# A convolution-gated layer with an MLP on one core: the order of two first loads, and the cut of the last output tile

## The chip, the cores and the metric

The kernel runs on one core of a Trainium2 chip. The metric is the device time of one execution in microseconds (us); the lower, the better. Each version is timed in several runs and the median is given. One execution is also profiled: the profile's times are counted from the start of its span, and "the profiled execution" below means that one.

## The reference

The inputs are one sequence of 2048 tokens with 512 channels (`A_q`, `A_k`, `A_v`), four tap weights for each channel (`A_shift_k`, 512 x 4), a long filter for each channel (`A_ssm_k`, 512 x 2048), a skip weight for each channel (`A_ssm_D`) and two MLP matrices (512 x 1376 and 1376 x 512), all bf16.

```python
kv = (sum over t of shifted k * shift_k) * v          # four taps along the sequence
y  = causal long convolution of kv with ssm_k          # FFT of length 4096 in the reference
h  = x + layernorm(x) * (y + kv * ssm_D)
h2 = h + relu(layernorm(h) @ w1) @ w2                  # output, 2048 x 512
```

## The kernel before

The long convolution is done as two-stage Fourier transforms by TensorE: the filter and `kv` are turned into rows of the first stage, multiplied by small sine matrices, combined stage by stage, multiplied pointwise and transformed back. The MLP follows in four blocks of 512 tokens. The program is written in one order by hand, and each engine takes its instructions strictly in that order, so an instruction that waits holds all that stand behind it on the same engine. Loads and stores are issued by SyncE (SP) and by ScalarE (ACT); each has a DMA queue of its own, and both queues run on the same 16 DMA engines.

**The start.** SP issues the load of the tap weights `wsh` (line 123: 4 KB, in 512 runs of 8 bytes), then the load of the long filter `sk` (line 124: 2 MB, in 512 runs of 4 KB), then eight transposing loads of k and v, alternately (lines 134 to 137). ACT issues two loads of `ssm_D` (line 128) and then loads its table of sines. TensorE (PE) runs 28 matmuls of zeros (line 156, `psz`), whose result nobody reads; they fill the time until `sk` is there. Then come 32 transposes of the filter (line 284, `pst`), in `to_rows` for h = 0 to 3. The first of them waits for `sk`. They are written as 8, 8, 8, 4 and 4; the results are copied out of PSUM (line 287 on ACT, line 289 on VectorE, DVE): the first, third and fourth group by ACT, the second and the fifth by DVE. The fifth group waits for DVE's copy of the second. Behind them stand the taps (line 335, `pkv`), matmuls against diagonal matrices `wdiag`, and the first Fourier stage (line 300).

**What stands behind the tap weights.** DVE's line 191 casts `wsh` to `wf` and waits for its load. Behind it on DVE, in this order: the phases of the small sine tables (lines 44 and 46, eight instructions in all; the fifth waits for nothing of the load but reads what POOL wrote), casts of the first table (lines 210 to 215), the phases of the large table (lines 222 and 220), small constants (lines 229 to 233), and then the copy of the second transpose group (line 289). On ACT: two sines (line 147) that need the phases, 16 products that make `wdiag` (line 204; they need `wf`), one more sine, and then the copies of line 287. POOL's line 246 reads `ssm_D`.

**The end.** `mlp2` (lines 664 to 681) makes one output tile of 128 tokens at a time: 11 matmuls (line 674), a DVE instruction that scales and adds (line 676), and a store issued by ACT (line 679). The last tile (t = 15) is made in two halves of 256 columns, each with its own 11 matmuls, DVE instruction and store. A store's destination is described as 4 x 32 rows.

Of the kernel before, what the change touches and what calls it, by code (L numbers as in the profile page):

```python
# [15 lines left out]
P = 128  # L16
# [40 lines left out]
def kernel(  # L57
# [13 lines left out]
    nc = tc.nc  # L71
    _, S, D = A_q.shape
# [3 lines left out]
    NT = 16  # L76
# [26 lines left out]
    def view(at, n, dt, t=E):  # L103
        return t[:, at:at + n].bitcast(dt)

    def small(shape, dt):
        n = math.prod(shape) * (2 if dt == BF16 else 4) // 4
        v = view(taken[0], n, dt)
        taken[0] += n
        return v.rearrange("p (a b) -> p a b", a=shape[0]) if len(shape) == 2 else v  # L110
# [9 lines left out]
    tsn = G[:, 2048:4096].rearrange("p (a b) -> p a b", a=32)  # L120

    wsh = consts.tile([P, DC, KS], BF16, name="wsh")
    nc.sync.dma_start(out=wsh[:], in_=A_shift_k.rearrange("(r p) j -> p r j", p=P))
    nc.sync.dma_start(out=sk, in_=A_ssm_k.rearrange("(c p) t -> p c t", p=P))
    draw = small([DC * P], BF16)
    for dp in range(2):
        src = bass.AP(tensor=A_ssm_D.tensor, offset=A_ssm_D.offset, ap=[[0, 1], [1, DC * P]])
# [536 lines left out]
    def mlp2(sc, hook=None):  # L664
        h1T = h1s[sc]
        for i in range(4):
            t = 4 * sc + i
            o = ob[t % 3]
            w = D // 2 if t == NT - 1 else D
            for d0 in range(0, D, w):  # L670
                ps2 = psm.tile([P, D], F32, tag="ps", name="ps2m")[:, 0:w]
                for fc in range(NFC):
                    ksz = min(P, DFF - fc * P)
                    nc.tensor.matmul(out=ps2, lhsT=h1T[:ksz, fc, i * P:(i + 1) * P], rhs=w2[:ksz, fc, d0:d0 + w],  # L674
                                     start=(fc == 0), stop=(fc == NFC - 1))
                nc.vector.scalar_tensor_tensor(out=o[:, d0:d0 + w], in0=ps2, scalar=rstd2[:, t, :], in1=xh[sc][:, i, d0:d0 + w],  # L676
                                               op0=ALU.mult, op1=ALU.add)
                dst = bass.AP(tensor=out_d.tensor, offset=out_d.offset + t * D + d0, ap=[[16 * D, 4], [64 * D, 32], [1, w]])
                nc.scalar.dma_start(out=dst, in_=o[:, d0:d0 + w])
            if hook is not None:  # L680
                hook(i)

# [20 lines left out]
    def next_norm(q):  # L703
# [7 lines left out]
        return hook  # L711

    mlp2(0, next_norm(2))
    inv2(2, psz)
    ec_wrap(3)
    mlp1(1, lambda fc: ec_sins(3, (fc // 3,)) if fc in (1, 4, 7, 10) else None)
    stats(xh[1], mv2, rstd2, 1)
    gate(2)
    mlp2(1, next_norm(3))
    inv2(3, psz)  # L720
    mlp1(2)
    stats(xh[2], mv2, rstd2, 2)
    gate(3)
    mlp2(2)
    mlp1(3)
    stats(xh[3], mv2, rstd2, 3)
# [32 lines left out]
```

## Time and profile before

| | us |
|---|---|
| median of 3 runs | 208.73 |
| lowest and highest | 208.56, 209.94 |
| the profiled execution's own time | 208.83 |
| span of its profile | 206.4 |
| PE busy | 198.7 (96%) |
| DVE busy | 141.8 (69%) |
| ACT busy | 117.3 (57%) |
| last matmul ends, by the chain of waits | 202.03 |
| last DVE instruction | 202.05 to 202.53 |

The span is what the profiler saw of the program; 2.4 us of the profiled execution's time lie around it. The profile's chain of waits follows the work that ended last back from the end; its pieces, put in order of time, tell which engine's work the end hung on at each moment. The timeline gives an instruction's start, its duration and, in brackets, how long its engine had been idle before it and what ended that. "SPq" and "ACTq" are the issuing of DMAs by these two engines.

### The profile page before, as it was taken

What the parts mean: (1) busy time and instruction counts of PE and PEld (TensorE: products, weight loads), DVE (VectorE), ACT (ScalarE), POOL (GpSimd) and SP (SyncE); (2) the same over time, 40 slices, a digit from 0 to 9 for tenths busy, and PEclk for the clock granted to TensorE, in tenths of its full rate; (3) what the DMA queues carried; (4) which work ended last, traced back from release to release, by engine and by line L of the source; (5) the groups of instructions that cost most, each with busy time, mean ns of one, the idle gap of its engine ahead of it and who ended that gap; (6) DMA issues with size and microseconds to landing.
All of it is one profiled execution on the core that took longest, in us unless ns stands there. A gap on an engine that the chain in (4) does not pass through costs nothing.

```text
span 206.4 us, 4344 instructions
## 1 busy us (share of the span) xinstructions
PE 198.7 (96%) x1733; PEld 138.3 (67%) x1741; DVE 141.8 (69%) x246; ACT 117.3 (57%) x190; POOL 69.5 (34%) x118
## 2 busy tenths in 40 slices
PE   8999999998999999999999999999999999999991
PEld 2575556877899998899998944466444844444450
DVE  5989898698689989997743775899079742261131
ACT  5776789787687787777692068403950065026300
POOL 7963801991555699232003032042202010002000
PEclk9999999999999999999999999999999999999997
DMA  5999990001600000035515999999906717110011
GB/s 147 353 205 168 203 162 6 0 5 21 258 0 0 3 0 3 0 105 102 96 35 180 229 224 121 212 145 134 114 17 118 161 25 91 42 56 17 0 51 51
DMA packets 47818, 19.91 MB, mean 96 GB/s; under 512 B 42710, under 2 KB 46264, under 8 KB 47800
## 3 DMA queue, kind: packets, MB, share of 16 engines
q1 hardware_dynamic: 44144, 16.15, 42.4%
q10 hardware_dynamic: 3656, 3.51, 6.0%
q8 instruction: 13, 0.21, 0.4%
q14 instruction: 5, 0.04, 0.1%
HBM read 7.02 MB, written 2.10 MB: 44 GB/s over the span
## 4 chain that ended last, share of the span: by engine, by line
PE 94%; DVE 2%; ACT 1%; issue 1%; ACTq 0%
PE ps1m L658 18%; PE ps2m L674 18%; PE psi L555 11%; PE u L433 8%; PE us L443 8%; PE ps L300 8%; PE pz L646 7%; PE pkv L335 7%; PE psz L156 4%; PE pst L284 4%; DVE BK L450 1%; ACT ktu L423 1%; ACT BX L273 0%; DVE BK L312 0%; ACT BK L315 0%
## 5 line engine op out<-in xcount | busy, mean ns | idle before, releaser
L660 ACT ACTIVATE M<-ps1m 128x512 bf16<-128x512 f32 (+1 forms) x44 | 25.1, 595 | 49.4 <-PE ps1m L658 28.1
L674 PE MATMUL ps2m<-M 128*128 128x512 bf16 (+3 forms) x183 | 38.5, 366 | 0.2
L674 PEld LDWEIGHTS <-M 128*128 128x128 bf16 (+1 forms) x187 | 18.3, 98 | 19.9
L658 PEld LDWEIGHTS <-w 128*128 128x128 bf16 (+1 forms) x176 | 17.4, 100 | 19.9
L383 POOL TENSOR_TENSOR smc<-st 64x256 fp32r<-64x256 f32 x32 | 22.8, 731 | 13.6 <-PE us L443 12.8
L517 POOL TENSOR_SCALAR rstd<-mv 128x4 f32<-128x4 f32 x8 | 2.2, 277 | 70.1 <-DVE mv L515 70.1
L676 DVE SCALAR_TENSOR_TENSOR M<-ps2m,rstd,M 128x512 bf16<-128x512 f32 (+1 forms) x13 | 9.1, 705 | 22.6 <-PE ps2m L674 13.5
L450 DVE TENSOR_TENSOR BK<-u,ktu 128x512 fp32r<-128x512 f32 x32 | 20.6, 685 | 4.9 <-PE us L443 2.7
L555 PE MATMUL psi<-inv,BK 128*128 128x128 f32 x128 | 21.1, 255 | 0.0
L423 ACT COPY ktu<-u 128x512 f32<-128x512 f32 x32 | 18.0, 588 | 5.1 <-DVE BK L450 2.4
L555 PE MATMUL psi<-inv,BX 128*128 128x256 f32 x64 | 20.5, 338 | 0.1
L555 PEld LDWEIGHTS psi<-inv,BK 128*128 128x128 f32 x128 | 19.7, 197 | 0.0
L658 PE MATMUL ps1m<-M,w 128*128 128x512 bf16 (+1 forms) x88 | 19.3, 379 | 0.0
L658 PE MATMUL ps1m<-xT,w 128*128 128x512 bf16 (+1 forms) x88 | 19.3, 379 | 0.0
L433 PE MATMUL u<-BK,st 64*128 64x256 f32 x128 | 14.2, 303 | 0.0
L433 PE MATMUL u<-BX,st 64*128 64x256 f32 x128 | 13.0, 283 | 0.0
L555 PEld LDWEIGHTS psi<-inv,BX 128*128 128x128 f32 x64 | 12.1, 196 | 0.4 <-DVE BK L450 0.4
L513 DVE BATCH_NORM_STATS2 st<-M 128x6 f32<-128x512 bf16 x20 | 12.3, 677 | 0.0
L315 ACT CAST BK<-ps 128x512 fp32r<-128x512 f32 x16 | 9.3, 585 | 5.0 <-PE ps L300 3.4
L632 DVE TENSOR_TENSOR qT<-pz,qT 128x2048 bf16<-128x2048 f32 x2 | 4.6, 2291 | 10.7 <-DMA qT<-M 6.5
L443 PE MATMUL us<-BK,smc 128*128 128x256 f32 x64 | 10.8, 294 | 0.7 <-ACT BX L273 0.6
L450 DVE TENSOR_TENSOR BX<-us,kts 128x512 fp32r<-128x512 f32 x16 | 10.9, 685 | 0.8
(126 smaller groups left out, 405.5 us busy)
## 6 DMA issues: line engine op xcount, KB each, us to landing
E<-in_A_ssm_k_dram SPq DMA_DIRECT2D x1, 2048.0 KB
out_dram<-M ACTq DMA_DIRECT2D x15, 128.0 KB
w<-in_B_w_dram SPq DMA_DIRECT2D x1, 1376.0 KB
M<-in_B_w_dram ACTq DMA_DIRECT2D x1, 1280.0 KB
M<-in_A_q_dram SPq DMA_DIRECT2D x8, 128.0 KB
xh<-in_A_q_dram SPq DMA_DIRECT2D x4, 128.0 KB
xr<-in_A_q_dram SPq DMA_DIRECT2D x4, 128.0 KB
out_dram<-M ACTq DMA_DIRECT2D x2, 64.0 KB
```

The lines of the kernel that those rows point to most:

```text
L300: nc.tensor.matmul(out=pss[rp][:, gi // 2, :, gi % 2, :], lhsT=fl[rows, 2 * g:2 * g + 2, :].rearrange("p d n -> p (d n)"), rhs=f[rows].rea ...
L335: nc.tensor.matmul(out=ps[:, i, :], lhsT=wdiag[:, r0 + i, j, :], rhs=kT[c][:, r0 + i, 16 - j:CH + 16 - j], start=(j == 0), stop=(j == KS - 1))
L383: nc.gpsimd.tensor_tensor(out=smc[pq, c % 3, i, :, 64 * dp:64 * dp + 64], in0=st[pq, ks, 64:128].bitcast(F32), in1=st[pq, ks, 0:64].bitcas ...
L423: nc.scalar.copy(out=kt[:], in_=ps)
L433: nc.tensor.matmul(out=ps[:, dp, 256 * x:256 * x + 256], lhsT=t[pq], rhs=cols((BK, BX)[x], pq, k1, i), start=(i == 0), stop=(i == 1), tile ...
L443: nc.tensor.matmul(out=ps[:, k % 2, 256 * x:256 * x + 256], lhsT=smc[:, k // 4 % 3, i, k % 4, :], rhs=cols((BK, BX)[x], slice(0, P), k, i) ...
L450: nc.vector.tensor_tensor(out=o, in0=ps[:, :, 256:512].rearrange("p b (g x) -> p b g x", x=8), in1=kt[:].rearrange("p b (g x) -> p b g x", ...
L555: nc.tensor.matmul(out=o if part == 0 else o[:, P * part - P:P * part], lhsT=src[:, g // 2, :, g % 2::2].rearrange("p c r -> p (c r)"), rh ...
L646: nc.tensor.matmul(out=pz[:, i, :, a:a + w, :].rearrange("p (s r) a n -> p s r (a n)", s=2), lhsT=ax[rho][:, n2 // 2, n2 % 2, :], rhs=ecor ...
L658: nc.tensor.matmul(out=ps1[:fsz, :].rearrange("p (i t) -> p i t", i=4), lhsT=w1[:, c, fc * P:fc * P + fsz], rhs=hT[sc][:, :, c, :], start= ...
L660: nc.scalar.activation(out=h1T[:fsz, fc, :], in_=ps1[:fsz, :], func=ACT.Relu)
L674: nc.tensor.matmul(out=ps2, lhsT=h1T[:ksz, fc, i * P:(i + 1) * P], rhs=w2[:ksz, fc, d0:d0 + w], start=(fc == 0), stop=(fc == NFC - 1))
```

## The change

```diff
     wsh = consts.tile([P, DC, KS], BF16, name="wsh")
-    nc.sync.dma_start(out=wsh[:], in_=A_shift_k.rearrange("(r p) j -> p r j", p=P))
     nc.sync.dma_start(out=sk, in_=A_ssm_k.rearrange("(c p) t -> p c t", p=P))
+    nc.scalar.dma_start(out=wsh[:], in_=A_shift_k.rearrange("(r p) j -> p r j", p=P))
     draw = small([DC * P], BF16)
...
             o = ob[t % 3]
-            w = D // 2 if t == NT - 1 else D
-            for d0 in range(0, D, w):
+
+            for d0, w in ((0, 384), (384, 128)) if t == NT - 1 else ((0, D),):
                 ps2 = psm.tile([P, D], F32, tag="ps", name="ps2m")[:, 0:w]
...
-                nc.scalar.dma_start(out=dst, in_=o[:, d0:d0 + w])
+                (nc.scalar if d0 == 0 else nc.sync).dma_start(out=dst, in_=o[:, d0:d0 + w])
```

At the start, SP's first issue is now the long filter, and the tap weights are the first issue of ACT, ahead of the two `ssm_D` loads and of the table load. At the end, the last tile is cut into 384 and 128 columns in place of 256 and 256; the store of the second piece is issued by SP. The number of matmuls, DVE instructions and stores is the same, and so is the order on PE, DVE and POOL.

## The prediction

> **What bounds the kernel now.** I read the chain of waits first. Its columns are start, duration and work:
>
> ```profile
> 0.98 8.67 PE psz L156 x28
> 9.66 3.23 PE pst L284 x28
> 12.89 0.04 issue
> 12.93 0.72 PE pst L284 x4
> ...
> 192.74 9.29 PE ps2m L674 x53
> 202.03 0.02 issue
> 202.05 0.48 DVE M L676
> ```
>
> PE carries the chain from 0.98 us to 202.03 us, so a change at the start pays or costs only through PE. The 28 matmuls of zeros run until about 9.5 us whatever the loads do. Next the timeline of each engine for the start:
>
> ```profile
> 0.72 0.46 SPq L123 DMA_DIRECT2D wsh<-in_A_shift_k_dram  x1
> 1.25 0.48 SPq L124 DMA_DIRECT2D E<-in_A_ssm_k_dram  x1
> ...
> 2.77 0.17 DVE L191 CAST wf<-wsh 128x16 f32<-128x16 bf16 x1 [0.69 <-DMA wsh<-in_A_shift_k_dram]
> ...
> 3.62 1.98 DVE L44 TENSOR_SCALAR E<-E,n2c 128x64 int32<-128x64 int32 x1
> ...
> 5.74 0.25 DVE L44 TENSOR_SCALAR E<-E,n2c 128x64 int32<-128x64 int32 x1
> ...
> 11.67 1.21 DVE L289 TENSOR_SCALAR E<-pst 128x1024 int32<-128x1024 int32 x1
> ...
> 12.93 0.53 PEld L284 LDWEIGHTS pst<-identw,E 128*128 128x128 f32 x4 [0.23 <-DVE E L289]
> ```
>
> The reader is to see a second chain. DVE waits 0.69 us for the tap weights, then is busy without a break from 2.77 to 12.88, and PE's last four transposes wait for that end: PE and DVE arrive together. One gap is hidden in it: the first L44 on 64 columns took 1.98 us and its twin 0.25, because POOL's iota (3.61 to 5.55) was in its way; 1.73 us of slack. On ACT:
>
> ```profile
> 3.38 0.32 ACT L147 ACTIVATE E<-E,nbias 128x32 f32<-128x32 int32 x1 [0.53 <-DVE E L46]
> ...
> 10.69 1.01 ACT L287 COPY E<-pst 128x1024 f32<-128x1024 f32 x1 [1.66 <-PE pst L284]
> ```
>
> ACT has 1.66 us to spare before the first copy. So tap weights that arrive up to 1.66 us later, at 4.4 in place of 2.77, cost nothing; later than that, nearly each us costs one. Last, the busy time by windows; the last two columns are the DMA engines' mean busy share and GB/s:
>
> ```profile
> 1.80:2.40 0.60, 0.60 (x3) 0.30 (x2) 0.15 (x1) 0.60 (x1) 0.53 (x5) 1.00 0.50 9
> 3.80:8.40 4.60, 4.60 (x17) 1.83 (x16) 4.42 (x15) 4.60 (x17) 4.43 (x15) 1.00 1.01 413
> 202.00:203.40 1.40, 0.01 (x1) 0.00 (x0) 0.48 (x1) 0.00 (x0) 0.00 (x0) 1.00 0.26 84
> 203.40:204.90 1.50, 0.00 (x0) 0.00 (x0) 0.00 (x0) 0.00 (x0) 0.00 (x0) 0.69 0.28 85
> ```
>
> In 1.8 to 2.4 the tap weights pass nearly alone (their 512 packets of 8 B lie at 1.83 to 2.39 in the trace's packet records). From 3.8 to 8.4 the filter fills all 16 DMA engines; its 512 packets of 4 KB, 32 for each engine, take 159 ns each once under way, the last at 8.84. At the end a quarter of the DMA engines work without a pause from 201.6 to 204.95.
>
> **Part 1, the filter issued first.** Its issue moves from 1.25 to 0.72, so its last packet goes from 8.84 to 8.3. Its consumer, the first transpose, still stands behind the zeros: their last matmul starts at 9.28 and the first transpose at 9.52, a spacing of 0.24 against the regular 0.213. Gain 0.03 us at most; I take 0. The k and v transposing loads behind it on SP move 0.5 us forward; their consumers (line 335 at 13.49, line 338 at 15.43) show no DMA wait, so that is worth 0.
>
> **Part 2, the tap weights by ACT.** Three issues in place of two, 0.81 us for two, put the table load back by about 0.4: it ends at 3.26 in place of 2.85, still before the sine at 3.38. Worth 0, and 0.4 at most would fall on ACT's 1.66. The `ssm_D` loads behind it have time until POOL's line 246 at 6.57.
>
> What decides is the landing. Until now the taps' packets were through before the filter's first at 2.45. Now both are issued within 0.01 us on two queues over the same 16 engines: the filter's first packets would start at 0.72 + 1.20 = 1.92, the bulk of the taps' at 2.06 (1.34 after issue, as before). Bounds: the small packets slip through at once and land at 2.8, or they are served behind the filter. The nearest rows on two queues at once are the load of w2 by ACT (issued 110.12) and the transposes by SP (issued 110.92). SP's issue there took 6.00 us where the one at 124.21, with no other queue at work, took 1.94, and the packet records show none of its packets until 115.5, by when 1158 of w2's 1376 were through; a lone transpose at 171.63 moved its first at 172.75, 1.1 us after issue. So the queue that began 0.8 us later was starved for over 3 us. I take that end.
>
> [...]
>
> The price of that end: the taps land with the filter's last packet, 8.3, plus 0.38 us to the consumer (before: 2.39 to 2.77), so line 191 starts at 8.7. From there to the end of DVE's line 289 it was 10.11 us (2.77 to 12.88); less the 1.73 that hid behind POOL, and 0.34 of one line 46 that took 0.53 for 0.19 behind POOL's memset, 8.04. So line 289 ends at 16.75, and PE's fifth group starts at 16.8 in place of 12.93: **3.9 us**. ACT agrees: 8.7 + 6.26 (2.77 to 9.03) ends its third sine at 14.96, and its copies (1.01, then 1.50) end about 17.5, before the taps' matmuls need them. All later work hangs on PE and shifts with it.
>
> In those 3.9 us PE is idle, and its clock may fall. Rows: after the last matmul, at 202.03, the granted clock falls from 1.00 at 203.97, after 1.9 us; and at the start the weight loads of the zeros come every 0.43 us from 0.97 to 6.04, then every 0.213. So slow stretches exist and cost up to half of 5.07, 2.5 us; the lower bound is 0, if the clock holds. I take the middle, **1.3**.
>
> [...]
>
> **Part 3, the last tile.** PE: 11 x 384 + 11 x 128 columns is the same work as 22 x 256; the second group takes 0.59 us at half of 256's 107 ns, or 1.08 if each waits for a weight load of 98 ns. The last DVE instruction is shorter: 0.75 us for 512 columns and 0.48 for 256 give 0.35 for 128. So it ends at 202.40, or 202.89, against 202.53. But the stores set the end: tile 14's packets run from 201.6 to 203.39, then those of the first half to 204.19 and of the second to 204.95, with no pause. After the change the 384-column piece is issued at 202.1 and ready, 1.15 later as before, at 203.25, and the 128-column piece at 203.6 to 204.1: both while the same engines are busy. Packets (128 each) and bytes are unchanged, so the end stays at 204.95. Bounds: 0.3 us gained if the second queue overlaps, 0.2 lost if its first packets are as slow as those of 201.4 to 202.0 (24 GB/s). I take 0, and 0.49 us of weight loads hide under the stores; without that cover they would cost that.
>
> [...]
>
> **Sum.** 208.83 + 0 + 3.9 + 1.3 + 0 = 214.0; the profiled execution is 0.1 over the median, so **213.9**. Its own range is 211.5 (taps land at 7.6, clock holds) to 215.5 (full clock price).
>
> **The rivals.**
> - *The taps slip through* (not slower): in 2.4 to 3.8 the filter still moves slowly (75, then 169 GB/s), and the `ssm_D` load on ACT's queue landed amid the taps' packets without harm. If the engines let small packets pass there, they land at 2.8 to 4.4, all slack holds, and only parts 1 and 3 are left: **208.7**, from 208.3 to 209.0. It decides at a landing of 4.4. Here too the filter's head start buys nothing, since the zeros end when they ended. Against it: the starved transposes. Chance 0.36.
> - [...] Chance 0.10. [...]
> - *The forecast*: chance 0.54.
>
> **How the numbers follow.** A measurement of this kernel tells about 1%, 2.1 us, from no change. The forecast (0.54) lies wholly above, and I count 0.06 of the in-between case with it, so slower has 0.60; the slip-through case and the rest of the in-between give 0.39 to the same; 0.01 of the slip-through case is for faster, since no part is worth 2 us. The forecast alone has 0.54, so the range must take in the rivals: 208.3 to 215.5.
>
> **What would show it.** Line 191 on DVE starting near 8.7 (forecast) or under 4.4 (slip-through); the idle time before the fifth transpose group on PE (3.9 us, or 0.04); matmuls of line 335 at 0.43 us spacing behind it (the clock); stores still busy to about 2.4 us after the last DVE instruction. I am wrong if line 191 starts early, or starts late and PE does not idle.

## The result, and the profile after

The changed kernel takes 216.31 us (median of 6 runs, 216.01 to 217.59), the kernel before 209.14 in 6 runs (208.56 to 209.94). The ratio is 1.0363, 95% interval 1.0343 to 1.0384: slower by 3.6%. The direction and the place are those of the forecast; the time lies above its range, which ended at 215.5. The profiled execution took 216.38 us, 7.55 us more than before's; its span is 214.2 in place of 206.4.

The timeline of the changed kernel, DVE first, then POOL and PE (start, duration, instruction; in brackets the idle time before it and its end):

```profile
9.14 0.17 DVE L191 CAST wf<-wsh 128x16 f32<-128x16 bf16 x1 [7.07 <-DMA wsh<-in_A_shift_k_dram]
...
9.99 0.26 DVE L44 TENSOR_SCALAR E<-E,n2c 128x64 int32<-128x64 int32 x1
...
15.62 1.44 DVE L233 TENSOR_SCALAR esc<-rows,rof 128x4 f32<-128x4 f32 x1
16.97 0.22 DVE L233 TENSOR_SCALAR ebi<-rows,rof 128x4 f32<-128x4 f32 x1
17.11 1.21 DVE L289 TENSOR_SCALAR E<-pst 128x1024 int32<-128x1024 int32 x1
...
14.14 2.91 POOL L248 TENSOR_SCALAR G<-G,n2c 128x2048 int32<-128x2048 int32 x1 [1.69 <-DVE G L222]
...
18.37 1.12 PE L284 MATMUL pst<-identw,E 128*128 128x128 f32 x4 [5.71 <-DVE E L289]
...
20.14 2.76 PE L335 MATMUL pkv<-E 128*128 128x512 bf16 x6 [0.22 <-issue]
```

Line 191 waits 7.07 us for the tap weights, where it waited 0.69. From its start DVE works without a break to the end of line 289 at 18.32, and PE has waited 5.71 us for that. The first L44 on 64 columns, 1.98 us before, now takes 0.26: the slack behind POOL's iota is used up. One thing is new: the first line 233 takes 1.44 us where it took 0.28, and ends as POOL's line 248 does, at 17.05. In the kernel before, line 233 was through when line 248 began:

```profile
11.29 0.28 DVE L233 TENSOR_SCALAR esc<-rows,rof 128x4 f32<-128x4 f32 x1
...
11.84 1.98 POOL L248 TENSOR_SCALAR G<-G,n2c 128x2048 int32<-128x2048 int32 x1
```

Behind the stall PE is slow: its six matmuls of line 335 took 1.46 us before and take 2.76.

The chain of waits now names the load itself:

```profile
0.73 8.39 DMA wsh<-in_A_shift_k_dram
12.66 1.30 DVE G L222
13.98 1.23 DVE G L220
15.62 1.44 DVE esc L233
17.19 1.14 DVE E L289
18.37 1.12 PE pst L284 x4
20.14 2.76 PE pkv L335 x6
23.90 1.84 PE pkv L335 x8
```

The same chain in the kernel before:

```profile
12.93 0.72 PE pst L284 x4
...
13.92 1.46 PE pkv L335 x6
15.38 1.00 PE ps L300 x32
16.38 1.84 PE pkv L335 x8
```

Windows of the changed kernel (length, busy time by engine, then the granted clock, the DMA share and GB/s):

```profile
3.40:8.40 5.00, 5.00 (x19) 2.07 (x18) 0.00 (x0) 0.10 (x1) 2.89 (x6) 1.00 1.04 378
12.70:14.60 1.90, 0.00 (x0) 0.00 (x0) 1.86 (x2) 1.90 (x8) 0.46 (x1) 1.00 1.06 174
14.60:18.40 3.80, 0.03 (x1) 0.03 (x1) 3.61 (x8) 3.80 (x7) 2.44 (x1) 0.68 1.20 221
18.40:21.50 3.10, 2.88 (x9) 1.63 (x11) 1.83 (x2) 1.10 (x1) 0.00 (x0) 0.50 1.01 180
21.50:22.90 1.40, 1.40 (x6) 0.28 (x6) 0.00 (x0) 0.00 (x0) 0.00 (x0) 0.54 1.26 279
...
210.80:212.30 1.50, 0.00 (x0) 0.00 (x0) 0.00 (x0) 0.00 (x0) 0.00 (x0) 1.00 0.27 75
212.30:212.80 0.50, 0.00 (x0) 0.00 (x0) 0.00 (x0) 0.00 (x0) 0.00 (x0) 1.00 0.21 47
```

Read the PE column and the clock together: no PE work from 12.7 on, the clock down to 0.5 within 14.6 to 18.4, and still 0.5 until shortly before 22.9, over 4 us of PE work. The mean of 0.68 over 3.80 us puts the fall near 16.0, some 3.3 us after PE's last transpose. In the last two windows the stores move 75 and 47 GB/s where before they moved 85.

Where the 7.55 us lie, read at points that both traces have. The fifth transpose group starts at 18.37 against 12.93: 5.44. The next tap block (line 335, eight matmuls) starts at 23.90 against 16.38, 7.52 later, so 2.08 were lost behind the stall: the last four transposes took 1.12 for 0.72, and from there to the first stage it was 3.41 us for 1.73. From the last matmul to the last store packet it is 3.26 us (209.51 to 212.77) in place of 2.92 (202.03 to 204.95): 0.34. That makes 7.86. In between 0.03 of it is regained, which leaves the difference of the spans, 7.83; and what lies outside the span is 0.28 shorter, which leaves 7.55.

### The profile page after: what moved, and what is told of

Read it like the earlier page. It is cut to its first block, busy times and chain, and to the rows that moved or that the text cites. A ratio compares the mean times of both kernels' runs of the same rounds, so it can differ in the third digit from the quotient of the medians.

```text
span 214.2 us, 4344 instructions
## 1 busy us (share of the span) xinstructions
PE 200.4 (94%) x1733; PEld 138.6 (65%) x1741; DVE 140.8 (66%) x246; ACT 117.0 (55%) x190; POOL 68.3 (32%) x118
## 3 DMA queue, kind: packets, MB, share of 16 engines
HBM read 7.02 MB, written 2.10 MB: 43 GB/s over the span
## 4 chain that ended last, share of the span: by engine, by line
PE 85%; DVE 6%; DMA 4%; ACT 2%; issue 1%; DVEq 0%; ACTq 0%
PE ps1m L658 18%; PE ps2m L674 17%; PE psi L555 11%; PE u L433 8%; PE us L443 8%; PE ps L300 7%; PE pkv L335 7%; PE pz L646 7%; DMA wsh<-in_A_shift_k_dram 4%; PE pst L284 2%; DVE esc L233 1%; DVE BK L450 1%; DVE G L222 1%; DVE G L220 1%; ACT ktu L423 1%
## 5 line engine op out<-in xcount | busy, mean ns | idle before, releaser
L674 PE MATMUL ps2m<-M 128*128 128x512 bf16 (+4 forms) x183 | 38.5, 366 | 0.2
L676 DVE SCALAR_TENSOR_TENSOR M<-ps2m,rstd,M 128x512 bf16<-128x512 f32 (+2 forms) x13 | 9.2, 707 | 22.7 <-PE ps2m L674 13.8
L284 PE MATMUL pst<-identw,E 128*128 128x128 f32 x64 | 8.3, 287 | 5.7 <-DVE E L289 5.7
L338 DVE TENSOR_TENSOR E<-pkv,E 128x1024 bf16<-128x1024 f32 (+1 forms) x9 | 9.8, 1102 | 3.6 <-PE pkv L335 3.6
L284 PEld LDWEIGHTS pst<-identw,E 128*128 128x128 f32 x64 | 7.7, 194 | 6.2 <-DVE E L289 5.9
```

The costliest lines, as they stand in the source:

```text
L284: nc.tensor.transpose(out=pst[:, i, :], in_=srcw[:, :, 8 * h + i0 + i], identity=identw[:])
```

## The experiments

**Which part of the change.** `start_only` has the start of the change and the tile cut of before; `tail_only` the reverse.

```diff
# start_only
-    nc.sync.dma_start(out=wsh[:], ...)
     nc.sync.dma_start(out=sk, ...)
+    nc.scalar.dma_start(out=wsh[:], ...)
# tail_only
-            w = D // 2 if t == NT - 1 else D
-            for d0 in range(0, D, w):
+            for d0, w in ((0, 384), (384, 128)) if t == NT - 1 else ((0, D),):
...
-                nc.scalar.dma_start(out=dst, in_=o[:, d0:d0 + w])
+                (nc.scalar if d0 == 0 else nc.sync).dma_start(out=dst, in_=o[:, d0:d0 + w])
```

> Only the start of the change: filter issued first by SP, tap weights by ACT; last tile as before. Theory: the whole loss but the stores' 0.3 us is here, +7.2 us over the kernel before (stall of the fifth transpose group 5.4, slow clock behind it 2.1, less what lies outside the span). Rival: the new cut of the last tile costs a good part, then this is under +5.5 us.

> Only the end of the change: last tile in 384 and 128 columns, second store by SP. Theory: +0.3 us over before, since SP's store starts its packets 2 us after its issue and the first piece has more to move; from the last matmul's end to the last packet 3.26 us in place of 2.92. Rival (the prediction's): 0, within 0.1 us.

`start_only`: 216.57 us, ratio 1.0366 (1.0329 to 1.0404). `tail_only`: 209.15 us, ratio 1.0020 (1.0001 to 1.0038), about 0.4 us. The loss is the start's, all but a few tenths; it is 7.6 to 7.8 us there, more than the 7.2 I had expected.

**What delays the taps.** Five kernels vary how the two loads meet. `taps_behind` puts both on SP, the filter first. `taps_lead` lets SP issue both `ssm_D` loads ahead of the filter, and `lead_half` one of them, with the taps first on ACT's queue. `start_8pk` and `start_16pk` are `start_only` with the taps read in fewer, longer runs, which go to other channels. The edits are against the kernel before; its own two issues are removed where they are issued anew.

```diff
# taps_behind
     nc.sync.dma_start(out=sk, ...)
+    nc.sync.dma_start(out=wsh[:], ...)
# lead_half (taps_lead: both ssm_D loads by nc.sync)
+    nc.scalar.dma_start(out=wsh[:], ...)
+    (nc.sync, nc.scalar)[dp].dma_start(out=draw[64 * dp:64 * dp + 1, :], in_=src)    # dp = 0, 1
     nc.sync.dma_start(out=sk, ...)
# start_8pk
+    nc.scalar.dma_start(out=wsh[:], in_=A_shift_k.rearrange("(p r) j -> p r j", p=P))
# start_16pk
+    nc.scalar.dma_start(out=wsh[:].rearrange("p (r q) j -> p r (q j)", q=2), in_=A_shift_k.rearrange("(r p q) j -> p r (q j)", p=P, q=2))
```

> Both loads on SP, the filter first and the tap weights behind it on the same queue. Theory: the taps wait for all filter packets of their engine, then pass in 0.3 us; line 191 starts at 8.6 to 9.0, the loss is as in start_only or up to 0.5 us less. Rival (it is the second queue that makes the taps late): they land clearly earlier than in start_only, by over 1 us.

> Tap weights first on ACT's queue, and SP issues the two small ssm_D loads before the filter, so that the filter is issued some 0.8 us later than the taps; nothing else changed. Theory (what counts is the filter's packets beside the taps', not whose queue they are on): taps land by 2.8 us as before, filter at about 9.5, the time within 0.6 us of before. Rival (a load by ACT's queue lands late in itself): line 191 starts well after 4 us and the time rises with it.

> As start_only, with the tap weights read as 128 packets of 32 bytes in place of 512 of 8 bytes (8 for each DMA engine in place of 32); the taps so go to other channels and the output differs. Theory, the two queues take turns packet for packet: the taps are through after 8 filter packets of each engine in place of 32, so line 191 starts near 5 us, the stall is under 1 us, PE's clock does not fall, and the time is within 1 us of before. Rival, the later queue waits until the filter's is empty: line 191 still starts near 9 us and the time stays at +7.

> As start_only, with the tap weights as 256 packets of 16 bytes (other channels' taps, so another output). With 128 packets all of them passed at 1.77 to 2.08 us, ahead of the filter's second packets; with 512 none passed before 3.3. Theory (a race: what reaches an engine's queue before the filter's packets fill it passes, the rest takes one turn for one filter packet): some engines lose the race, line 191 starts between 3 and 6 us, and the time is under +1.5 us of before. Rival (the number of packets sets a fixed share of the filter's time): half of 512's, line 191 near 5.5. A landing under 2.8 or over 8 contradicts both.

> Taps as 512 packets first on ACT's queue; SP issues one small ssm_D load ahead of the filter, so the filter is issued some 0.3 us after the taps (0.66 in taps_lead, 0 in start_only). Theory (a race of some tenths of a us): line 191 under 4 us and the time as before within 0.5 us, or, if 0.3 us is too little, near 9 us with the full loss; a landing between would mean turns from the middle on. Rival (any filter packet issued before the taps are through delays them by its own time): line 191 later by at most 0.4 us per us of overlap, never near 9.

The landings, from the packet records and the timelines:

| | taps issued, filter issued | taps' packets | filter's packets | line 191 starts | time, ratio to before |
|---|---|---|---|---|---|
| before | 0.72, 1.25 | 1.83 to 2.38 | 2.45 to 8.68 | 2.77 | |
| start_only | 0.73, 0.72 | 3.30 to 8.48 | 1.86 to 8.25 | 9.18 | 216.57, 1.0366 |
| taps_behind | 1.25, 0.72 | 7.55 to 8.58 | 1.86 to 8.24 | 9.21 | 216.56, 1.0358 (1.0311 to 1.0405) |
| start_16pk (256 packets) | 0.73, 0.72 | 3.12 to 6.16 | 1.87 to 8.26 | 6.80 | 212.98, one run |
| start_8pk (128 packets) | 0.73, 0.72 | 1.77 to 2.08 | 1.86 to 8.32 | 2.53 | 208.73, 0.9988 (0.9970 to 1.0006) |
| lead_half | 0.73, 1.12 | 1.84 to 2.34 | 2.22 to 8.47 | 2.74 | 208.5, one run |
| taps_lead | 0.73, 1.39 | 1.82 to 2.38 | 2.47 to 8.60 | 2.81 | 209.07, 1.0008 (0.9983 to 1.0033) |

(Each packet time is the start of a packet, in the one profiled execution of each kernel; the one-run times stand beside a before of 209.36 in that group of runs.) The line that carries the reading of `start_16pk`, by the timeline:

```profile
6.80 0.17 DVE L191 CAST wf<-wsh 128x16 f32<-128x16 bf16 x1 [4.72 <-DMA wsh<-in_A_shift_k_dram]
```

and of `lead_half`, by the same view:

```profile
2.74 0.17 DVE L191 CAST wf<-wsh 128x16 f32<-128x16 bf16 x1 [0.66 <-DMA wsh<-in_A_shift_k_dram]
```

Four things follow for these runs. ACT's queue is not at fault: `taps_lead` (ratio 1.0008) and `lead_half` (208.5 us beside 209.36) use it and lose nothing. Being behind the filter in the same queue is no better: line 191 starts at 9.21 in `taps_behind`, at 9.18 in `start_only`. On two queues, issued together, the packets of the two loads take turns, one for one: in the changed kernel, from 4.0 to 7.5 us, each half microsecond holds 43 to 51 packets of the taps and 43 to 50 of the filter. Of the 332 taps' packets there, 320 start 3 or 4 ns before one filter packet ends and end 3 or 4 ns after the next begins, so each stands between two filter packets. Half as many packets (`start_16pk`) need 3.0 us in place of 5.2. And who came first decided: with the filter issued 0.4 us after the taps (`lead_half`) their packets started by 2.34, as before; with it issued at the same moment (`start_only`) the last started at 8.48; and of packets issued with it, 128 had all started by 2.08 where 256 and 512 began at 3.12 and 3.30. Why the turns begin only at 3.1 to 3.4 us, when the filter's packets begin at 1.9, and whether the 128 packets pass by their number or by their longer runs, no run here shows.

My expectations missed here. For `start_8pk` I had eight turns and line 191 near 5 us; its packets passed before the turns began. For `start_16pk` I had line 191 between 3 and 6 us and under +1.5 us of time. It started at 6.80, no packet passed early, and the time rose by 3.6 us. The rival, half of the landing of 512 packets, had 5.5; it is nearer, and misses because the turns begin only near 3.1. For `taps_behind` I had line 191 at 9.0 at the latest, and it started at 9.21.

**What the stall adds: clock and POOL.** `start_warm` gives PE more zeros, so that it works while DVE is late. `start_warm_consts` also takes DVE's small constants away from POOL's line 248. Neither changes what is computed.

```diff
# start_warm (start_warm_consts: 50)
-    fill(bank2("psz")[:, 0, :], 28)
+    fill(bank2("psz")[:, 0, :], 53)
# start_warm_consts: lines 224 to 233 ahead of these two
     nc.vector.tensor_single_scalar(out=tsn, in_=r2, scalar=n2c[:], op=ALU.mult)
     wrap13(tsn)
```

> start_only with 53 matmuls of zeros in place of 28, so that PE works while it would wait; its transposes start at about 14.6 us and its wait before the fifth group shrinks from 6 us to about 0.5. Theory (the slow clock behind the stall costs 2.1 us): the time falls by about 2.1 us from start_only, to a ratio of 1.026 over before, with line 335 at its usual 0.213 us spacing. Rival (the clock costs nothing, other engines set the pace behind the stall): no change, 1.036.

> start_only with DVE's small constants (lines 229 to 233) ahead of the large table's phases (lines 222, 220), and 50 matmuls of zeros. Theory (DVE's line 233 lost 1.16 us to POOL's line 248, which ran beside it): line 233 takes 0.28 us again, the fifth group starts 1.1 to 1.2 us earlier than in start_only, and with the clock kept the time falls by about 3.2 us from start_only, to a ratio of 1.021. Rival (the 1.16 us only moves to another DVE instruction beside POOL's): as start_warm, 1.026.

`start_warm`: 213.68 us, ratio 1.0213 (1.0190 to 1.0237). `start_warm_consts`: 212.13 us, 1.0141 (1.0111 to 1.0171). Their before is 209.36, that of `start_only` 208.77, so ratios are compared: 1.5 points for the clock, 0.7 for the constants. The timeline of `start_warm`, on PE:

```profile
15.16 3.76 PE L284 MATMUL pst<-identw,E 128*128 128x128 f32 x32
18.76 1.89 PE L335 MATMUL pkv<-E 128*128 128x512 bf16 x7
```

The 32 transposes run in one piece and the matmuls of line 335 keep their pace, seven in 1.89 us as in the kernel before. Its span is 211.7, that of `start_only` 213.6: 1.9 us, near the 2.1 read above. Timed, it is 2.9 to 3.2, more than I had expected. The profiled execution of `start_only` is the shortest of its four: their spans are 213.6 to 214.5, those of `start_warm` 211.4 to 211.7, which is 2.5 us in the mean.

The granted clock differs between the executions too. In the four profiles with a stall it falls to half and returns at these times:

| | clock full from | falls to half | is full again | PE works again from | half of the time from there to the full clock |
|---|---|---|---|---|---|
| changed kernel | 5.72 | 15.96 | 22.79 | 18.37 | 2.2 |
| start_only | 4.93 | 15.17 | 22.00 | 18.47 | 1.8 |
| taps_behind | 6.51 | 16.75 | 23.57 | 18.21 | 2.7 |
| start_16pk | 5.35 | 15.59 | 19.00 | 16.02 | 1.5 |

In all four the clock is full for 10.24 us; it is then at half for 6.82 or 6.83 us, in `start_16pk` for 3.41. These are three, two and one times 3.41 us; what sets them no run here shows. In the changed kernel the matmuls of line 335 start 0.43 us apart at half clock and 0.213 in the kernel before at full clock, so PE loses half of the time that it works at half clock. By an estimate from these times (the last column) the four stalls cost 1.5 to 2.7 us in clock; read in the trace of the changed kernel it was 2.1.

`start_warm_consts` bears on line 233. On DVE, first in `start_warm`, then in `start_warm_consts`, where the same instruction is line 231:

```profile
15.94 1.47 DVE L233 TENSOR_SCALAR esc<-rows,rof 128x4 f32<-128x4 f32 x1
```

```profile
13.35 0.23 DVE L231 TENSOR_SCALAR esc<-rows,rof 128x4 f32<-128x4 f32 x1
```

The copy behind it, in `start_warm_consts`:

```profile
16.08 1.95 DVE L289 TENSOR_SCALAR E<-pst 128x1024 int32<-128x1024 int32 x2
```

Line 289 starts at 16.08, 1.37 us before `start_warm`'s 17.45, of which 0.14 is its earlier taps; the span falls by another 1.5 to 210.2. That is 3.8 us over before's 206.4, with the landing late and both additions gone. So the time that line 233 lost beside POOL is real and was on the path. Lines 220 and 289 beside the same POOL instruction, which ran from 15.09 to 18.01, keep their durations: 1.23 us for line 220, and 1.95 for the two of line 289, which take 1.21 and 0.69 apart in `start_warm`. In the changed kernel line 220 began 0.16 us ahead of POOL's line 248, which then took 2.91 us where it took 1.98 before, and line 233 began while line 248 ran. Why line 233 is held up there and line 289 is not, no run here shows.

**The last tile.** `tail_act` has the new cut with both stores by ACT, `tail_256_sp` the old cut with the second store by SP. `tail_four` keeps the old cut and splits each store of the last two tiles into four of 32 tokens.

```diff
# tail_four, for t >= 14
+                    for a in range(4):
+                        dst = bass.AP(tensor=out_d.tensor, offset=out_d.offset + (16 * a + t) * D + d0, ap=[[64 * D, 32], [1, w]])
+                        (nc.scalar, nc.sync)[a % 2].dma_start(out=dst, in_=o[32 * a:32 * a + 32, d0:d0 + w])
```

> 384 and 128 columns, both stores by ACT. Theory (SP's late first packets are the cost): 0 within 0.1 us of before, packets without a pause. Rival (the cut itself costs, as the first store has more bytes and is ready later): +0.2 to +0.3 as in tail_only.

> 256 and 256 columns as before, the second store by SP. Theory (SP's late first packets): +0.2 to +0.4 us, its packets begin 2 us after its issue. Rival (the cut is the cost): 0 within 0.1.

> The kernel before, with each store of the last two tiles made as four of 32 tokens each, in turn by ACT and SP, so that the destination's outer dimension is 32 in place of 4. Theory (the end hangs on stores that a quarter of the DMA engines carry): the packets spread over all 16 engines, the last one ends 0.4 to 0.7 us earlier, the time falls by 0.2 to 0.3 per cent. Rival (issuing four stores costs what the engines gain): no gain, or up to 0.5 us lost.

| | us | ratio (interval) |
|---|---|---|
| tail_only: 384 + 128, second by SP | 209.15 | 1.0020 (1.0001 to 1.0038) |
| tail_act: 384 + 128, both by ACT | 209.23 | 1.0018 (1.0004 to 1.0033) |
| tail_256_sp: 256 + 256, second by SP | 208.76 | 0.9991 (0.9977 to 1.0005) |
| tail_four | 207.98 | 0.9951 (0.9934 to 0.9968) |

So SP's queue costs nothing that the times show, and my theory of its late packets falls; the cut is the cost. The packet records give the size. In `tail_act` the 128 packets of 768 bytes start from 203.62 to 205.06 and those of 256 bytes from 204.78 to 205.54: 1.92 us from the first to the last, where the kernel before's 256 packets of 512 bytes take 1.55. Most of it lies in the large packets. Four packets of 4 bytes follow each store; I take them for one from each of the engines at work, an estimate from the DMA engines' share of 0.26 to 0.28 of 16 there. Behind the 512-byte stores of the kernel before all four come within 0.07 us, 0.8 us after the store's first packet. Behind the 768-byte store of the changed kernel two come after 1.2 us, about what 768 bytes for 512 would make of 0.8, and two after 1.5. Why two are late no run here shows. `tail_four` shows the other side. Its windows:

```profile
201.40:202.00 0.60, 0.58 (x6) 0.27 (x3) 0.00 (x0) 0.00 (x0) 0.00 (x0) 1.00 0.63 147
202.00:203.40 1.40, 0.00 (x0) 0.00 (x0) 0.48 (x1) 0.00 (x0) 0.00 (x0) 1.00 0.26 58
203.40:204.90 1.50, 0.00 (x0) 0.00 (x0) 0.00 (x0) 0.00 (x0) 0.00 (x0) 1.00 0.18 39
```

Where the kernel before moved 24, 84 and 85 GB/s in windows of the same bounds, this one moves 147, 58 and 39: tile 14's bytes are out early, at a share of 0.63 of the DMA engines in the first window where the kernel before had 0.17, and its last store packet starts at 204.1 in place of 204.9. At 207.98 us it is faster than both kernels, by 0.5% over before, more than the 0.2 to 0.3% I had written down. It changes three things at once, the outer dimension, the number of stores and the second queue; the last alone, in `tail_256_sp`, gave nothing, and the other two were not separated.

## Why the prediction was wrong in size

- **Part 1, the filter first, worth 0.** Right: its packets end near 8.3, and the first transpose starts at 9.35 for 9.52.
- **Part 2, the landing.** Nearly right in size, by another mechanism: line 191 at 8.7 forecast, 9.14 measured. The precedent it was argued from, a starved queue, was not what happened (and of w2's 1376 packets 1108 were through by 115.5, not 1158). The queues took turns, packet for packet: 320 of 332 taps' packets stood between two of the filter's. They came to the same end because the taps have as many packets as the filter, 512, and that was luck: with half as many, the last packet started 2.3 us earlier. Of the 0.44 us that line 191 came later than forecast, 0.1 is the last packet, which started at 8.42; the rest lies between it and line 191, 0.72 us in place of 0.38. The `ssm_D` loads did not have the time that they were given: POOL's line 246 waited 2.88 us for them, to 9.23. That cost nothing, since POOL then still waited 1.69 us for DVE's line 222.
- **Part 2, the path behind it: the step that failed.** "From there to the end of DVE's line 289 ... 8.04" assumed that DVE's instructions keep their durations when they move. They took 9.18, 1.14 more, and line 233's 1.16 beside POOL's line 248 is that difference. POOL's instruction waits for DVE's line 222, so it moved with it, and met other instructions than before. With line 233 out of its way, in `start_warm_consts`, the same stretch took 7.96 (9.33 to 17.29). The stall was put at 3.9 and is 5.44; with the landing that is the whole of it.
- **Part 2, the clock.** Forecast 1.3 as a middle of 0 to 2.5, measured 2.08 in the trace. Mis-sized: the row at the end of the profile, where the clock falls 1.9 us after the last matmul, spoke for a fall within a stall of 3.9, and the middle set it half aside. In the changed kernel the clock fell 3.3 us after PE's last transpose, and was full again 4.4 us after PE's next.
- **Part 3, the last tile, worth 0.** That packets and bytes are unchanged, and so the end stays, failed: with as many packets and bytes, the uneven cut took 1.92 us for its packets where the even one takes 1.55. Measured +0.34 us in the trace, +0.2% alone. That PE's second group is no slower (0.61 us measured, 0.59 forecast) and that SP's queue brings nothing was right.
- **The rivals.** The slip-through case is what happened with a lead of 0.4 us or with 128 packets: landings that let line 191 start at 2.5 to 2.8 cost nothing (208.5 us beside 209.36, and ratios 0.9988 and 1.0008). Whether its bound of 4.4 is right is not shown, since in no run line 191 starts between 2.8 and 6.8. The in-between case, a landing between slip-through and forecast with a chance of 0.10, is `start_16pk`: by the prediction's price, nearly one us for each after 4.4, line 191 at 6.80 would cost 2.4 us. It cost 3.6: PE idled 3.54 us, and the clock fell to half at 15.59, 3.1 us after PE's last work; there too DVE's path took 9.2 us, and line 233 1.44. The forecast's case, held at 0.54, is the one that came.
- **The range** ended at 215.5, where 208.83, 3.9 and 2.5 make 215.2; the prediction does not say for what the rest is. It added the upper clock price to a stall taken at one value, and left the bounds of the landing, of DVE's path and of the stores out of its upper end. 0.44, 1.14, 0.78 and 0.34 us add up to 2.7, less the 0.28 outside the span.

## What to carry to other kernels

In these runs a lead over a large load was enough for a load of 512 tiny packets: 0.4 us on a second queue (`lead_half`), 0.5 on the same one (the kernel before). Issued at the same time on two queues, its packets took turns with the large load's, and in the changed kernel its last started at 8.42 us, behind the large load's last at 8.19, since that one had 512 too. When a wait is priced by shifting a chain, look again at what runs beside each instruction at its new place (line 233 took 1.44 us for 0.28), and at whether PE, idle meanwhile, loses its clock (here from 1.00 to 0.50, 3.3 us after its last work). The stores at the end did not cost by bytes alone here: an uneven cut of the last tile cost 0.2%, and splitting the last two tiles' stores in four, on two queues, gave 0.5%.

## What the runs showed of the hardware that was not expected

- 128 packets of 768 bytes and 128 of 256 took 1.92 us from first to last on the stores' engines, where 256 of 512 bytes take 1.55. Of the four packets of 4 bytes behind the 768-byte store of the changed kernel, two came 0.3 us after the other two; behind the 512-byte stores of the kernel before all four came within 0.07.
- With the same 28 matmuls of zeros the first transpose started anywhere from 9.06 (`start_8pk`) to 9.99 us (`taps_lead`), 9.52 before and 9.35 after. The clock became full at 4.96, 7.02, 6.00 and 5.72 us in them: 2.06 us more at half clock, 0.93 us later. That this is what spreads a kernel's times over 0.5% was not tried.
- In the four profiles with a stall the clock's changes are 10.24 and then 6.83 or 3.41 us apart, and in the kernel before it fell at 203.97, 197.97 us after it became full at 6.00, which is 58 times 3.413. It fell 2.7 to 3.7 us after PE's last work in the stalls (3.3 in the changed kernel) and 1.9 us after it at the end of the kernel before, and came back after some 4.4 us of work at half pace in the changed kernel and 3.0 us in `start_16pk`.
